# Attention and mixture-of-experts kernel: another order of score tiles, exponentials and routing tasks, and another buffer for one result

## The chip, the core and the metric

The kernel runs on one core of one Trainium2 chip, in a single launch. TensorE (PE) multiplies matrices into PSUM, ScalarE (ACT) applies tanh, exp, relu and casts, VectorE (DVE) and GpSimd (POOL) do elementwise work, and DMA queues are issued by SyncE (SP), ACT and POOL. The metric is the device time of the launch in microseconds (us); lower is better. A profile gives the span of one execution, engine by engine.

## The reference

Inputs are q, k, v of 8 batches x 12 heads x 448 tokens x 64, and a mixture of 8 experts over 3584 tokens of 768. All numbers are float32.

```
scores = cap * tanh((q @ k.T / 8) / cap)           # cap = 30
attn   = softmax(scores);  x = attn @ v            # 3584 x 768
logits = x @ w_gate;  e = argmax(logits)           # one expert for each token
out[t] = softmax(logits)[e] * (relu(x[t] @ w1[e]) @ w2[e])
```

## The kernel before

**Attention** works on pairs of heads. Step `n` of the loop (lines 1027 to 1059) takes pair `n` of 48; six steps are a batch, and two steps (an even one and the odd one behind it) share one load of q, k and v. The 448 keys of a pair are cut into three units of 128 and a rest of 64. The rests of an even pair and of the odd pair behind it fill one tile together, which the even step makes. `scores(n, half)` multiplies a unit's keys by the queries into a PSUM tile `sp` (L248; the rest at L260), of which there are two, so that a unit can't start before the tanh of the unit two ahead of it has ended. ACT puts the tanh into `pt` (L249) or, for the rest, into `pr` (L263), and then takes the exponential in place: units 0 and 1 at once (L266, 1792 columns), unit 2 alone (L266, 896 columns), the rest alone (L268). Half 0 is units 0 and 1; half 1 is unit 2 and, in even steps, the rest.

**Values.** `pv(n, half)` multiplies the exponentials by v into PSUM tiles `po0` (even pairs) and `po1` (odd pairs). It is called one step later than the scores: `pv(n-1, 0)` behind `scores(n, 0)`, and `pv(n-1, 1)` behind `scores(n, 1)`. For an even pair, its half 0 begins with the rest's matmuls for both pairs (L300), so in an odd step PE first does two units of scores, then L300, then L310 for units 0 and 1, then the sums of the softmax (L341), then unit 2, then L310 for unit 2. DVE copies `po` to `ot` (L319). `adds(n, half)` adds up the exponentials in `p4`: two additions on DVE (L277) and, for the rest, one on POOL (L285).

**Routing.** Behind each batch its softmax sums and its gate logits are worked off in the next batch's steps. With `n` the batch's last step plus one, a table of tasks (`at(step, when, f)`, L971 to L1022) says in which step and at which of the places 0, 5, 3, 6, 1, 2 of the loop's body each stands: `rec_v` (reciprocals, DVE), `rec_p` (PE, L396), `rec_c`, `log_v` (scaled logits `lr`, DVE, L410 to L424), `log_p` (PE, L429, sums them over partitions), `route_v` (first maximum and one-hot `ob`, DVE, L449 to L463), `route_s` (exp on ACT, L469), `place_p` (PE, L500 and L502), `route_g` (DVE, L474 to L481), `scale` and `store` of the rows into `xd` in DRAM, and `place_d`, which scatters token numbers (POOL, L527). The body's order is: loads, `turn`, 0, `scores(n, 0)`, `pv(n-1, 0)`, 5, `adds(n, 0)`, `scores(n, 1)`, 3, `pv(n-1, 1)`, 6, `adds(n, 1)`, 1, 2. Each engine runs its own instructions in the order written.

**The first expert block.** The largest expert's first block takes tokens of batches 0 to 3 only, so its rows are gathered from `xd` into `xg` during steps 37 to 43, three and one in turn and two at the end (L1007 to L1010, POOL, L750). DVE transposes them (`trans_x`, L858) from the end of step 44 on, and ACT and DVE split them into two parts.

**The experts.** Then come blocks in the order of `ORDER`: six of 448 tokens (large) and two of 256 (small). For each, `up` multiplies by w1 (L884), ACT and DVE make the hidden part `hb` (L889, L890), `down` multiplies by w2 (L908 large, L916 small), `evac` copies the sums from PSUM to `ys` (L934 large; L942 on ACT and L944 on DVE small), and `put` scatters `ys` to the output (POOL, L760). `ys` is one buffer for all blocks: `evac` of a block waits until the scatters of the block before have read it. For a small block all of the block before is scattered at once (L1257), 14 scatters if that one was large. The rows of the next block are gathered into `xg` while a block runs, transposed at its end, and `xg` has no further use after the last block's transposes.

Of the kernel before, what the change touches and what calls it, by code (L numbers as in the profile page):

```python
# [4 lines left out]
F32 = mybir.dt.float32  # L5
# [4 lines left out]
AF = mybir.ActivationFunctionType  # L10
# [15 lines left out]
KM = 384  # L26
# [98 lines left out]
def attention_moe(tc, qT, kT, vL, capd, wgL, w1a, w1b, w2a, w2b, cst, cmk, out):  # L125
# [110 lines left out]
    def scores(n, half):  # L236
        qr, kr, _ = raws[n // 2]
        i = n % 2
        if half == 0:
            probs[n] = pb.tile([128, 6, S], F32, name="pt", bufs=2)  # L240
        pt = probs[n]
        for g in (0, 1) if half == 0 else (2,):
            sp = ps_s.tile([128, 2, 512], F32, name="sp")
            c = slice(128 * g, 128 * g + 128)

            for j in range(2):
                r = slice(64 * j, 64 * j + 64)
                PE.matmul(sp[:, j, 0:S], kr[r, i, c], qr[r, i, :], start=True, stop=True)  # L248
            A.activation(out=pt[:, 2 * g : 2 * g + 2, :], in_=sp[:, 0:2, 0:S], func=AF.Tanh, scale=qsc)  # L249
            if n == g == 0:  # L250
                A.activation(out=pt[:, 0:2, :], in_=pt[:, 0:2, :], func=AF.Exp, scale=capt)
        rest = half == 1 and i == 0
        if rest:

            sp = ps_s.tile([128, 2, 512], F32, name="sp")
            pr = rests[n // 2] = pb.tile([128, 2, S], F32, name="pr", bufs=2)
            for i in range(2):
                for j in range(2):
                    r = slice(64 * j, 64 * j + 64)
                    PE.matmul(  # L260
                        sp[64 * i : 64 * i + 64, j, 0:S], kr[r, i, KM:S], qr[r, i, :], start=True, stop=True
                    )
            A.activation(out=pr, in_=sp[:, 0:2, 0:S], func=AF.Tanh, scale=qsc)  # L263

        for lo, hi in ((0, 4) if half == 0 else (4, 6),) if n else ((2, 4), (4, 6))[: 2 * half]:
            A.activation(out=pt[:, lo:hi, :], in_=pt[:, lo:hi, :], func=AF.Exp, scale=capt)  # L266
        if rest:
            A.activation(out=pr, in_=pr, func=AF.Exp, scale=capt)  # L268

# [20 lines left out]
    def pv(n, half):  # L290
# [3 lines left out]
        if half == 0 and n % 2 == 0:  # L294

            for i in range(2):
                pvs[n + i] = ps_o.tile([128, 512], F32, name=f"po{i}")
                r = slice(64 * i, 64 * i + 64)
                for j in range(2):
                    PE.matmul(  # L300
                        pvs[n + i][64 * j : 64 * j + 64, 0:S],
                        vr[r, 12 + j, :],
                        rests[n // 2][r, j],
                        start=True,
                        stop=False,
                    )
        po = pvs[n]
        for t in (0, 1) if half == 0 else (2,):
            for j in range(2):
                PE.matmul(  # L310
                    po[64 * j : 64 * j + 64, 0:S],
                    vr[:, n % 2 * 6 + 3 * j + t, :],
                    pt[:, 2 * t + j],
                    start=False,
                    stop=t == 2,
                )
# [609 lines left out]
    def evac(j, cs=range(2)):  # L926
        y = m["y"]
        if cs[0] == 0:
            ys[j] = ys0 if j < 0 else m["yo"].tile([128, QB * XW], F32, name="ys")
# [41 lines left out]
    for b in range(B):  # L971
# [13 lines left out]
        at(n + 3, 3, log_p, b)  # L985
        at(n + 3, 6, route_v, b)
        at(n + 4, 0, route_s, b)
        at(n + 4, 3, place_p, b)
        at(n + 4, 0, route_g, b)
# [37 lines left out]
    for n in range(n_pairs + 1):  # L1027
# [10 lines left out]
        if n > 0:  # L1038
            pv(n - 1, 0)
        do(n, 5)  # L1040
        if live:
# [3 lines left out]
            if n == 0:  # L1045
                adds(n, 0)
# [307 lines left out]
```

## Time and profile before

| | |
|---|---|
| median of three runs | 906.6 us (904.43 to 909.86) |
| the profiled execution | 905.34 us, of which the span is 903.6 us |
| mean granted clock of TensorE | 0.977 |
| VectorE busy | 548.7 us (61%) |
| ScalarE busy | 483.9 us (54%) |
| GpSimd busy | 466.0 us (52%) |

The span has three stages: attention up to about 340 us, a passage up to about 430 us in which attention's last steps overlap the first expert block, and the expert blocks up to the end. The expert blocks are ruled by TensorE; in attention TensorE and ScalarE are close to each other. Times in rows are microseconds from the span's start, a row being start, duration, engine, line, operation, output<-input, shapes and a count of merged instructions; what stands in brackets is the engine's idle time ahead of it and the instruction whose end released it.

### The profile page before, as it was taken

The page shows a single profiled execution, that of the slowest core. Times are in us where ns is not written, and L with a number is a line of the kernel's source. Part 1 is how long each engine was busy: PE and PEld are TensorE (multiplying, and loading weights), DVE is VectorE, ACT ScalarE, POOL GpSimd, SP SyncE. Part 2 cuts the span into 40 slices and gives each one's busy share as a digit, 9 for nine tenths or more (in the row PEclk, how much of TensorE's full clock was granted, in tenths as well). Part 3 has the DMA queues.
Part 4 walks back from the last instruction along what each step waited for, and adds up shares of the span by engine and source line. Part 5 has one row for each costly group of instructions (what it writes and reads, how often), then busy time and mean ns, then how long its engine had stood idle before and what let it go on. Part 6 is the DMA issues. An engine that isn't in the chain of part 4 may idle for free. (4 is left out here: it accounts for less than half of the span.)

```text
span 903.6 us, 12040 instructions
## 1 busy us (share of the span) xinstructions
PE 838.4 (93%) x4492; PEld 557.4 (62%) x4492; DVE 548.7 (61%) x885; ACT 483.9 (54%) x573; POOL 466.0 (52%) x382
## 2 busy tenths in 40 slices
PE   8999999999999996786999999999999999999893
PEld 3222322222223221265989989899999999999893
DVE  3559797979797965777373763744735537356520
ACT  7988889888978883632332532332423324234410
POOL 1423353434343645653718857577577575665600
PEclk9999999999999997998999999999999999999997
DMA  5231545454527572404455312453431124444100
GB/s 202 70 123 62 182 65 181 65 181 66 180 97 210 173 246 89 64 16 126 154 202 193 127 27 62 180 188 128 169 127 53 32 64 176 183 177 173 65 34 33
DMA packets 45155, 111.67 MB, mean 124 GB/s; under 512 B 8561, under 2 KB 27411, under 8 KB 42016
## 3 DMA queue, kind: packets, MB, share of 16 engines
q1 hardware_dynamic: 28384, 50.72, 19.6%
q0 software_dynamic: 16416, 59.87, 18.8%
q8 instruction: 37, 0.61, 0.3%
q14 instruction: 30, 0.25, 0.1%
q10 hardware_dynamic: 288, 0.23, 0.1%
HBM read 101.40 MB, written 22.36 MB: 137 GB/s over the span
## 5 line engine op out<-in xcount | busy, mean ns | idle before, releaser
L285 POOL TENSOR_TENSOR p<-p,pr 64x896 f32<-64x896 f32 x46 | 103.4, 2248 | 206.7 <-DVE p L277 150.3
L889 ACT ACTIVATE hb<-ph 128x448 fp32r<-128x448 f32 (+1 forms) x69 | 34.9, 508 | 296.7 <-PE ph L884 208.1
L890 DVE SCALAR_TENSOR_TENSOR hb<-ph,hb 128x448 fp32r<-128x448 f32 (+1 forms) x69 | 39.3, 574 | 202.6 <-ACT hb L889 202.5
L249 ACT ACTIVATE pt<-sp,qsc 128x896 f32<-128x896 f32 x144 | 138.7, 997 | 35.0 <-PE sp L248 34.9
L750 POOL DMA_INDIRECT xg<-xd,xi x114 | 134.5, 1180 | 37.9 <-issue 30.4
L248 PE MATMUL sp<-qr,kr 64*128 64x448 f32 x576 | 136.9, 580 | 11.1 <-ACT pt L249 10.9
L266 ACT ACTIVATE pt<-pt,capt 128x1792 f32<-128x1792 f32 (+1 forms) x96 | 134.9, 1406 | 2.3
L310 PE MATMUL po<-pt,vr 128*64 128x448 f32 x576 | 132.4, 568 | 0.0
L760 POOL DMA_INDIRECT out<-ys,xi x98 | 107.9, 1101 | 29.2 <-issue 27.0
L248 PEld LDWEIGHTS sp<-qr,kr 64*128 64x128 f32 x576 | 47.8, 187 | 98.7 <-ACT pt L249 43.7
L277 DVE TENSOR_TENSOR p<-pt 128x896 f32<-128x896 f32 x48 | 58.3, 1214 | 48.9 <-ACT pt L266 48.9
L310 PEld LDWEIGHTS po<-pt,vr 128*64 128x64 f32 x576 | 33.5, 138 | 76.4 <-issue 74.4
L277 DVE TENSOR_TENSOR p<-p,pt 128x896 f32<-128x896 f32 x48 | 53.8, 1121 | 9.6 <-ACT pt L266 9.5
L864 ACT CAST xh<-xt 128x448 fp32r<-128x448 f32 (+1 forms) x54 | 27.2, 532 | 42.6 <-DVE xt L858 42.6
L527 POOL DMA_INDIRECT ids<-tok,slots x32 | 38.4, 1200 | 10.9 <-issue 6.3
L319 DVE COPY ot<-po 128x448 f32<-128x448 f32 x48 | 29.7, 619 | 20.7 <-PE po L310 20.5
L300 PE MATMUL po<-pr,vr 64*64 64x448 f32 x192 | 25.0, 565 | 15.1 <-ACT pr L268 14.2
L750 POOL DMA_INDIRECT w1r<-in_w1b,widx x8 | 11.1, 1382 | 46.1 <-DVE w17l L796 45.5
L858 DVE STREAM_TRANSPOSE xt<-xg 128x448 f32<-128x448 f32 (+1 forms) x54 | 30.3, 585 | 7.3 <-DMA xg<-xd,xi 6.4
L865 DVE TENSOR_TENSOR xl<-xt,xh 128x448 fp32r<-128x448 f32 (+1 forms) x54 | 28.8, 559 | 2.6 <-ACT xh L864 2.5
L934 DVE STREAM_TRANSPOSE ys<-y 128x448 f32<-128x448 f32 x36 | 19.8, 612 | 12.8 <-DMA out<-ys,xi 7.3
L300 PEld LDWEIGHTS po<-pr,vr 64*64 64x64 f32 x192 | 5.3, 131 | 33.2 <-ACT pr L268 31.5
(410 smaller groups left out, 1970.6 us busy)
## 6 DMA issues: line engine op xcount, KB each, us to landing
vr<-in_vL SPq DMA_DIRECT2D x24, 448.0 KB, 6.2
kr<-in_kT SPq DMA_DIRECT2D x23, 448.0 KB, 3.7
qr<-in_qT SPq DMA_DIRECT2D x23, 448.0 KB, 6.0
xd<-yt SPq DMA_DIRECT2D x20, 336.0 KB, 6.8
xd<-w2r SPq DMA_DIRECT2D x12, 336.0 KB, 5.8
xg<-xd,xi POOLq DMA_INDIRECT x114, 3.1
out<-ys,xi POOLq DMA_INDIRECT x98, 2.4
w1r<-in_w1a SPq DMA_DIRECT2D x4, 384.0 KB, 6.2
```

Source lines behind the costliest of these rows:

```text
L248: PE.matmul(sp[:, j, 0:S], kr[r, i, c], qr[r, i, :], start=True, stop=True)
L249: A.activation(out=pt[:, 2 * g : 2 * g + 2, :], in_=sp[:, 0:2, 0:S], func=AF.Tanh, scale=qsc)
L266: A.activation(out=pt[:, lo:hi, :], in_=pt[:, lo:hi, :], func=AF.Exp, scale=capt)
L277: V.tensor_tensor(out=p4, in0=pt[:, 0:2] if half == 0 else p4, in1=pt[:, 2 * half + 2 : 2 * half + 4], op=ALU.add)
L285: e.tensor_tensor(out=p4[r], in0=p4[r], in1=rests[n // 2][r], op=ALU.add)
L300: PE.matmul(pvs[n + i][64 * j : 64 * j + 64, 0:S], vr[r, 12 + j, :], rests[n // 2][r, j], start=True, stop=False,)
L310: PE.matmul(po[64 * j : 64 * j + 64, 0:S], vr[:, n % 2 * 6 + 3 * j + t, :], pt[:, 2 * t + j], start=False, stop=t == 2,)
L527: i = G.indirect_dma_start(out=ids, out_offset=bass.IndirectOffsetOnAxis(ap=slots[0:p, c : c + 1].bitcast(U32), axis=0), in_=tok[0:p, c : ...
L750: G.indirect_dma_start(out=dst, out_offset=None, in_=src, in_offset=bass.IndirectOffsetOnAxis(ap=idx.bitcast(U32), axis=0), bounds_check=b ...
L760: i = G.indirect_dma_start(out=dst, out_offset=bass.IndirectOffsetOnAxis(ap=idx.bitcast(U32), axis=0), in_=src, in_offset=None, bounds_che ...
L889: A.activation(out=hh, in_=ph, func=AF.Relu)
L890: V.scalar_tensor_tensor(out=hl, in0=ph, scalar=0.0, in1=hh, op0=ALU.max, op1=ALU.subtract)
```

## The change

There are four edits.

1. `scores`: in even steps other than step 0 the rest's scores, tanh and exponential come ahead of those of unit 2. In step 0 each unit's exponential follows its tanh at once, and the order is 0, 1, 2, rest.
2. `pv(0, 0)` is done in step 0 behind its scores, not in step 1; for pair 0 alone the rest's matmuls come last.
3. In the table, `log_p` goes from place 3 to place 6 of its step (behind `pv(n-1, 1)`), `route_v` from 6 to 1 (behind `adds(n, 1)`), `route_s` from 0 to 5 and `route_g` from 0 to 6 of the step after.
4. `evac` of the first small block (`ORDER[-2]`) writes into `xg` in place of `ys`.

```diff
@@ scores
-        for g in (0, 1) if half == 0 else (2,):
+        rest = half == 1 and i == 0
+        units = (0, 1) if half == 0 else (2,) if not rest else (3, 2) if n else (2, 3)
+        for g in units:
             sp = ps_s.tile([128, 2, 512], F32, name="sp")
...
+            A.activation(out=x, in_=sp[:, 0:2, 0:S], func=AF.Tanh, scale=qsc)
+            if n == 0:
+                A.activation(out=x, in_=x, func=AF.Exp, scale=capt)
+        if n == 0:
+            return
         if rest:
+            pr = rests[n // 2]
             A.activation(out=pr, in_=pr, func=AF.Exp, scale=capt)
+        lo, hi = (0, 4) if half == 0 else (4, 6)
+        A.activation(out=pt[:, lo:hi, :], in_=pt[:, lo:hi, :], func=AF.Exp, scale=capt)
@@ pv
+        if n > 0 and half == 0 and n % 2 == 0:
+            rest()
+        main()
+        if n == 0 and half == 1:
+            rest()
@@ evac
-            ys[j] = ys0 if j < 0 else m["yo"].tile([128, QB * XW], F32, name="ys")
+            ys[j] = (
+                ys0
+                if j == -1
+                else xg.rearrange("p q x -> p (q x)")
+                if j == ORDER[-2]
+                else m["yo"].tile([128, QB * XW], F32, name="ys")
+            )
@@ the table
-        at(n + 3, 3, log_p, b)
-        at(n + 3, 6, route_v, b)
-        at(n + 4, 0, route_s, b)
+        at(n + 3, 6, log_p, b)
+        at(n + 3, 1, route_v, b)
+        at(n + 4, 5, route_s, b)
         at(n + 4, 3, place_p, b)
-        at(n + 4, 0, route_g, b)
+        at(n + 4, 6, route_g, b)
@@ the loop
-        if n > 0:
+        if n > 1:
             pv(n - 1, 0)
...
             if n == 0:
+                pv(n, 0)
                 adds(n, 0)
```

The change moves instructions on three engines that wait for one another. On ACT, step 2 and the first two tanh of step 3 stood so before (L249 is a tanh of units, L263 the rest's tanh, L266 an exponential of units, L268 the rest's):

```order
L249 ACTIVATE pt<-sp,qsc 128x896 x2
L266 ACTIVATE pt<-pt,capt 128x1792
L249 ACTIVATE pt<-sp,qsc 128x896
L263 ACTIVATE pr<-sp,qsc 128x896
L266 ACTIVATE pt<-pt,capt 128x896
L268 ACTIVATE pr<-pr,capt 128x896
L249 ACTIVATE pt<-sp,qsc 128x896 x2
```

The same even step 2 on ACT now, in which L263 is every tanh, L270 the rest's exponential and L272 that of units:

```order
L263 ACTIVATE pt<-sp,qsc 128x896 x2
L272 ACTIVATE pt<-pt,capt 128x1792
L263 ACTIVATE pr<-sp,qsc 128x896
L263 ACTIVATE pt<-sp,qsc 128x896
L270 ACTIVATE pr<-pr,capt 128x896
L272 ACTIVATE pt<-pt,capt 128x896
L263 ACTIVATE pt<-sp,qsc 128x896 x2
```

The rest's exponential, which PE's first value matmuls of step 3 read, has moved one place ahead of unit 2's, and PE's scores (L260, L248) have changed places with it.

On PE, the odd step in which batch 0's `log_p` stands (step 9) and the step behind it began so before, from the sums on (L341 sums, L248 scores, L429 `log_p`, L310 values):

```order
L341 MATMUL ps_s<-p_464,cs 32x448 x2
L248 MATMUL sp<-qr,kr 128x448 x2
L429 MATMUL ps_l<-lr,cs 128x112
L310 MATMUL po_562<-pt,vr 64x448 x2
L248 MATMUL sp<-qr,kr 128x448 x4
```

The same place on PE now (L357 sums, L252 scores, L319 values, L445 `log_p`):

```order
L357 MATMUL ps_s<-p_464,cs 32x448 x2
L252 MATMUL sp<-qr,kr 128x448 x2
L319 MATMUL po_562<-pt,vr 64x448 x2
L445 MATMUL ps_l<-lr,cs 128x112
L252 MATMUL sp<-qr,kr 128x448 x4
```

`log_p` has moved behind unit 2's value matmuls, and so stands directly ahead of the next step's scores.

On ACT at the end of the first small block, before and then now, with what each waits for (a DMASW is a semaphore of DMAs that POOL issues, a DMAHW one of DMAs that SP issues; L864 and L880 split the last block's rows, L889 and L905 make `hb`):

```order
L864 CAST xh<-xt 128x256 [waits DVE_49] x6
L942 COPY ys<-y_6534 128x3x4x32 [waits DMASW6_49,DMASW5_49,DMASW7_49,DMASW4_49,DMAHW4_49,DMASW3_49,DMAHW5_49,DMASW2_49,DMAHW6_49,DMASW1_49,DMAHW7_49,DMASW0_49,PE_49]
L942 COPY ys<-y_6536 128x3x4x32 [waits PE_49]
L889 ACTIVATE hb<-ph 128x256 [waits PE_49,Activation_49] x2
L791 CAST w17h<-w1r_115 128x768
```

```order
L880 CAST xh<-xt 128x256 [waits DVE_49] x6
L965 COPY xg<-y_6534 128x3x4x32 [waits DMASW2_49,DMASW1_49,DMASW7_49,DMASW0_49,PE_49]
L965 COPY xg<-y_6536 128x3x4x32 [waits DMASW5_49,DMASW4_49,DMASW6_49,DMASW3_49,PE_49]
L905 ACTIVATE hb<-ph 128x256 [waits PE_49,Activation_49] x2
L807 CAST w17h<-w1r_115 128x768
```

The first copy waited for twelve DMA semaphores in one row; each of the two copies now waits for four, as many as the gathers that filled its half of `xg` for the last block.

More of the change, by code (lines that the diff above doesn't have):

```diff
@@ L241, in scores @@
         pt = probs[n]
-        for g in (0, 1) if half == 0 else (2,):
+        rest = half == 1 and i == 0
+        units = (0, 1) if half == 0 else (2,) if not rest else (3, 2) if n else (2, 3)
+        for g in units:
             sp = ps_s.tile([128, 2, 512], F32, name="sp")
[L244 to L257, printed above, removed]
+            if g < 3:
+                c = slice(128 * g, 128 * g + 128)
                 for j in range(2):
                     r = slice(64 * j, 64 * j + 64)
[L260 to L263, printed above, removed]
@@ L265, in scores @@
-        for lo, hi in ((0, 4) if half == 0 else (4, 6),) if n else ((2, 4), (4, 6))[: 2 * half]:
-            A.activation(out=pt[:, lo:hi, :], in_=pt[:, lo:hi, :], func=AF.Exp, scale=capt)
+                    PE.matmul(sp[:, j, 0:S], kr[r, i, c], qr[r, i, :], start=True, stop=True)
+                x = pt[:, 2 * g : 2 * g + 2, :]
+            else:
+                for k in range(2):
+                    for j in range(2):
+                        r = slice(64 * j, 64 * j + 64)
+                        PE.matmul(
+                            sp[64 * k : 64 * k + 64, j, 0:S], kr[r, k, KM:S], qr[r, k, :], start=True, stop=True
+                        )
+                x = rests[n // 2] = pb.tile([128, 2, S], F32, name="pr", bufs=2)
@@ L297, in pv, with rest @@
                 pvs[n + i] = ps_o.tile([128, 512], F32, name=f"po{i}")
+        po = pvs[n]
+        def rest():
+            for i in range(2):
                 r = slice(64 * i, 64 * i + 64)
@@ L303, in pv, with main @@
                         rests[n // 2][r, j],
-                        start=True,
-                        stop=False,
-                    )
[L307 to L316, printed above, removed]
+                        start=n + i > 0,
+                        stop=n + i == 0,
+                    )
+        def main():
+            for t in (0, 1) if half == 0 else (2,):
+                for j in range(2):
+                    PE.matmul(
+                        po[64 * j : 64 * j + 64, 0:S],
+                        vr[:, n % 2 * 6 + 3 * j + t, :],
+                        pt[:, 2 * t + j],
+                        start=n == t == 0,
+                        stop=t == 2 and n > 0,
+                    )
+        if n > 0 and half == 0 and n % 2 == 0:
[3 more added lines that the diff above has]
+            rest()
         if half == 1:
@@ L928, in evac @@
         if cs[0] == 0:
-            ys[j] = ys0 if j < 0 else m["yo"].tile([128, QB * XW], F32, name="ys")
+            ys[j] = (
[4 more added lines that the diff above has]
+                else m["yo"].tile([128, QB * XW], F32, name="ys")
+            )
         o = ys[j]
```

## The prediction

> **What bounds the kernel now.** I begin with the busy time of each engine by stage (start:end, length, then PE, PE's weight loads, DVE, ACT and POOL, granted clock, share of the DMA engines, GB/s).
>
> ```profile
> 22.00:340.00 318.00, 303.45 (x1756) 92.44 (x1754) 250.16 (x388) 278.60 (x263) 131.62 (x73) 0.99 0.47 137
> 430.00:850.00 420.00, 415.11 (x2109) 383.81 (x2109) 220.99 (x333) 146.03 (x233) 276.20 (x266) 1.00 0.37 132
> ```
>
> PE is the bound in both: 303.45 of 318 us in attention, 415.11 of 420 us in the experts. ACT is close in attention (278.60). The change takes no matmul away, so it can only win PE's idle time: 14.55 us in attention, and what lies outside these stretches. Next, who ends PE's waits from 22 to 342 us (total, times, longest):
>
> ```profile
> PE po L300 <- ACT pr L268: 11.6, 22, 0.8
> PE ps_l L429 <- DVE lr L424: 2.0, 3, 0.7
> PE po L300 <- DVE ot L319: 0.9, 1, 0.9
> ```
>
> These three are 14.5 us, all of it. The large one stands once in every two steps: the rest's value matmuls wait for the rest's exponential. One such pair of steps, from the timelines of PE and ACT:
>
> ```profile
> 31.75 1.01 ACT L249 ACTIVATE pt<-sp,qsc 128x896 f32<-128x896 f32 x1 [0.96 <-PE sp L248]
> 38.66 1.77 PE L248 MATMUL sp<-qr,kr 64*128 64x448 f32 x8
> 39.12 1.04 ACT L266 ACTIVATE pt<-pt,capt 128x896 f32<-128x896 f32 x1
> 40.06 1.03 ACT L268 ACTIVATE pr<-pr,capt 128x896 f32<-128x896 f32 x1
> 41.14 0.98 PE L300 MATMUL po<-pr,vr 64*64 64x448 f32 x8 [0.71 <-ACT pr L268]
> 45.67 1.01 ACT L249 ACTIVATE pt<-sp,qsc 128x896 f32<-128x896 f32 x1 [0.97 <-PE sp L248]
> 46.45 1.77 PE L248 MATMUL sp<-qr,kr 64*128 64x448 f32 x8
> 48.16 1.73 PE L310 MATMUL po<-pt,vr 128*64 128x448 f32 x8
> ```
>
> The period, 31.75 to 45.67, is 13.92 us, a loop through both engines: ACT works without a gap from unit 2's tanh of the odd step (31.75) to the end of the rest's exponential (41.09), PE then needs until 45.67 to give it the next odd unit 2. Alone, each would be faster. Two units of scores take PE 1.71 us to their follower when nothing waits (46.45 to 48.16), here 2.48 (38.66 to 41.14): a wait costs 0.77, its printed 0.71 plus 0.06. So PE's own period is 13.15, and ACT's 13.92 - 0.96 = 12.96.
>
> **The change part by part.** *The rest ahead of unit 2.* Its exponential ends 0.94 us earlier (40.06 - 39.12), more than the longest wait (0.8 printed). The loop falls to 12.98, below PE's own 13.15, so PE paces. The second scores tile of the odd step now waits for unit 2's tanh; as the second of the two tanh it ends where the rest's did, so that wait is as long as before. ACT keeps 0.19 us of slack in a period: the whole wait goes, but only just. How far that holds, these rows of the same wait say:
>
> ```profile
> 280.75 0.98 PE L300 MATMUL po<-pr,vr 64*64 64x448 f32 x8 [0.44 <-ACT pr L268]
> 295.41 0.98 PE L300 MATMUL po<-pr,vr 64*64 64x448 f32 x8 [0.31 <-ACT pr L268]
> 310.01 0.98 PE L300 MATMUL po<-pr,vr 64*64 64x448 f32 x8 [0.77 <-ACT pr L268]
> 324.63 0.98 PE L300 MATMUL po<-pr,vr 64*64 64x448 f32 x8 [0.44 <-ACT pr L268]
> 339.40 1.11 PE L300 MATMUL po<-pr,vr 64*64 64x448 f32 x8 [0.31 <-ACT pr L268]
> 290.81 2.10 POOL L285 TENSOR_TENSOR p<-p,pr 64x896 f32<-64x896 f32 x1 [7.66 <-DVE p L277]
> 300.54 1.69 POOL L750 DMA_INDIRECT xg<-xd,xi  x1 [0.16 <-issue]
> 307.95 2.08 POOL L285 TENSOR_TENSOR p<-p,pr 64x896 f32<-64x896 f32 x1 [5.72 <-DMA xg<-xd,xi]
> 344.25 1.00 POOL L750 DMA_INDIRECT xg<-xd,xi  x1 [0.30 <-issue]
> 347.16 0.65 DVE L858 STREAM_TRANSPOSE xt<-xg 128x448 f32<-128x448 f32 x1 [6.44 <-DMA xg<-xd,xi]
> ```
>
> From step 37 (POOL's addition at 290.81) on, POOL alternates additions with the 14 gathers for the first expert block; the additions of odd steps wait until the gathers ahead have landed (5.72 us at 307.95). Its last gather is issued at 344.25, and DVE stands idle for 6.44 us until the rows are there at 347.16. So 290.81 to 347.16 (56.35 us) is a chain of POOL and DMA: what PE gains behind 291 us is lost in DVE's wait. The chain's start hangs on DVE's addition in step 37, which PE paces, so earlier gains pass. That leaves 22 waits less the last four: 11.6 - 0.31 - 0.77 - 0.44 - 0.31 = 9.8, and 18 x 0.06 = 1.1 beside them, **10.9 us**.
>
> *Unit 2's exponential later, and `log_p` later.* DVE's second addition of an even step now starts 0.8 to 0.9 us later, and three steps behind a batch DVE's `log_v` and PE's L429 follow it. The step of batch 1:
>
> ```profile
> 113.32 1.07 DVE L277 TENSOR_TENSOR p<-p,pt 128x896 f32<-128x896 f32 x1
> 114.16 0.98 PE L300 MATMUL po<-pr,vr 64*64 64x448 f32 x8 [0.31 <-ACT pr L268]
> 115.31 2.10 POOL L285 TENSOR_TENSOR p<-p,pr 64x896 f32<-64x896 f32 x1
> 115.52 2.77 DVE L419 TENSOR_TENSOR lt<-lt,rr 64x448 f32<-64x448 f32 x2
> 119.32 0.47 PE L429 MATMUL ps_l<-lr,cs 128*128 128x112 f32 x2 [0.69 <-DVE lr L424]
> 296.75 1.02 DVE L419 TENSOR_TENSOR lt<-lt,rr 64x448 f32<-64x448 f32 x2
> ```
>
> L419 takes 1.02 us alone and 2.77 beside POOL's addition: it ends 0.88 us after that does (118.29, 117.41). POOL's addition starts 0.17 us behind DVE's, here 115.4 instead of 115.31, because POOL was late anyway. So `lr` is ready at about 119.4 instead of 119.3. PE would reach the new place of L429 5.31 us after L300's start (41.14 to 46.45), and L300 starts at 113.79 without its wait: 119.10. A wait of about 0.3 stays of 0.75, in three batches: **+1.3 us** (at worst -0.3 each, at best +0.75 each). In batch 0, which had no wait, I expect POOL not late and so the 0.8 to 0.9 us to come through: a new wait of about 0.3, **-0.3** (ends 0 and -0.9). In step 33 DVE is behind for another reason:
>
> ```profile
> 249.97 1.31 PE L300 MATMUL po<-pr,vr 64*64 64x448 f32 x4 [0.91 <-DVE ot L319]
> 250.00:254.00 4.00, 4.00 (x12) 0.94 (x12) 3.95 (x6) 1.66 (x1) 2.07 (x1) 0.57 0.04 4
> ```
>
> PE waits until DVE has copied `po1`, so the 0.31 us won there is waited out again: **-0.4**. (The clock behind it was 0.57.) `route_v`, `route_s` and `route_g` stand behind instructions that others wait for, not ahead of them; what ACT waited for `route_s` lay in its slack of a period. I count nothing; the end is +0.5. In steps 45 to 47 DVE leads the passage: it no longer holds back an addition behind `route_v` but gets unit 2's exponential later in step 46; nothing, with ends -1 and +1.5.
>
> *Step 0.* ACT works without a gap there, and only the order in it changes: +0.2, ends 0 and 1.8 (PE's whole wait ahead of the first L300).
>
> *`xg` for `ys`.* The first small block's sums wait until 14 scatters of the large block before have read `ys`:
>
> ```profile
> 850.60 1.05 DVE L865 TENSOR_TENSOR xl<-xt,xh 128x256 fp32r<-128x256 f32 x3
> 851.97 0.28 PE L884 MATMUL ph<-xh,w10l 128*128 128x256 f32 x1
> 854.12 0.28 PE L884 MATMUL ph<-xh,w11l 128*128 128x256 f32 x1
> 856.79 0.86 ACT L942 COPY ys<-y 128x384 f32<-128x384 f32 x2 [5.67 <-DMA out<-ys,xi]
> 856.83 1.02 DVE L944 COPY ys<-y 128x384 f32<-128x384 f32 x2 [5.18 <-DMA out<-ys,xi]
> 858.00 0.67 PE L916 MATMUL y<-w20h,hb 128*128 128x384 f32 x1 [3.59 <-ACT hb L889]
> 858.00:862.00 4.00, 4.00 (x15) 4.00 (x16) 3.43 (x5) 2.40 (x4) 2.30 (x2) 0.57 0.41 162
> 858.00 3.92 PE y L916 x12
> 864.06 2.08 PE y L916 x12
> ```
>
> `xg` is free once the last block's rows are transposed, before 851.65 (the end of the splits). The copies then take DVE to 852.7, `hb` of the first `up` (matmuls until 852.25) is there by about 853.3, and PE, done with the second `up` at 854.24 (854.12 plus a matmul's spacing, 2.15 / 18 = 0.12), goes on at once: 858.00 - 854.24 = 3.76 us. After its wait the clock was 0.57, and twelve matmuls took 3.92 instead of 2.08: 1.84 more. What is late next is POOL's own pair of scatters, for which only the end waits, 30 us on. **5.6 us** in all; the lower end is 3.8.
>
> The Trainium skill, "TensorE: Matmul & The Clock Gate", Part 1: The HAM clock gate, says that the clock halves after an idle window of about 3.4 us and recovers after as long a busy one. The 3.59 us wait and the 0.57 agree. In step 33 the trace departs from it: waits of 0.31 and 0.91 us precede 0.57; by the page a short wait costs itself alone, and the sum would stay the same.
>
> The sum: 10.9 + 1.3 - 0.3 - 0.4 + 0.2 + 5.6 = 17.3 us, of 905.34 us for the profiled execution (span 903.6 and 1.74 around it): 888.0. The median of the runs is 1.3 higher, which gives 889.3; I say **888.6**.
>
> **The rivals.**
> *ACT takes the bound.* Its slack of 0.19 us a period is all there is: were its period 0.3 us over PE's, 18 periods would keep 5.4 us: 894. For: 278.60 busy of 318. Against: its waits for PE recur in every odd step.
> *POOL's gathers stretch or shrink.* Gathers took 1.69 us (300.54) or 1.00 (344.25). Were six more of the 14 slow because DVE is denser, 6 x 0.69 = 4.1 us come back: 892.7. Were the last rows to land 5 us sooner, PE would get most of DVE's 6.44: 884. The Trainium skill, "SBUF — State Buffer", SBUF: two separate sides, has a rule for the slow case: some DVE operations keep GpSimd from writing the descriptors of its own DMAs. The trace shows both durations but not which operation does it.
> *The chain doesn't move.* If its start hung on DMAs and not on DVE's step 37, attention's 11.7 would be lost: 900. Against: the row at 290.81 waited 7.66 us for DVE's addition, not for a DMA.
> *`xg` doesn't free the copies.* If the copies still waited for the scatters, 5.6 come back: 894. Against: they wait for fewer semaphores.
> *Slower.* L300 needs `po` copied by DVE. DVE's additions stand ahead of that copy and follow ACT, which now runs up to 0.8 us later against PE, so the copy could come late elsewhere, as in step 33. Price there: 0.91 us of wait and 4 us at a clock of 0.57, which lose 1.7: 2.6 us. From seven such steps on it eats 17.3 us; at fourteen, 36.4 - 17.3 = 19.1 slower, 926. Against: this wait stands once in 22 to 342 us.
>
> **How the numbers follow.** Forecast 0.66 (alone 884 to 893), ACT 0.10, gathers longer 0.06 or shorter 0.06, chain unmoved 0.05, copies not freed 0.04, slower 0.03. From 881 to 898 all but 900 and the slow case lie inside, with the ends of the unknown costs. A measurement of this kernel tells about 0.5% (4.5 us) from no change: only the last case is slower, a mishap of two of the others comes within: faster 0.94, same 0.03, slower 0.03.
>
> **What would show it.** PE's wait at L300 for the rest's exponential gone in all but the last steps, with the period at about 13.15; a wait of about 0.3 us at `log_p`; POOL's addition of step 37 near 279 us and still 56 us to the first transpose, DVE idle for 8 there; no wait of PE in the first small block and a clock of 1.00 behind it. The forecast fails if ACT's wait at odd unit 2 is gone while PE still waits, if POOL's 56 us change by over 4, or if PE waits for `ot` in more than one step.

## The result, and the profile after

The changed kernel takes **893.59 us** (median of 4 runs, 891.80 to 894.99), the kernel before in the same set 905.99 us (904.43 to 909.86): a ratio of 0.9847, 95% interval 0.9821 to 0.9872. The profiled execution takes 893.83 us with a span of 892.0, so 11.6 us of span are gone where the prediction had 17.3; by the medians it is 12.4. Line numbers have moved: scores L248 and L260 are now L252 and L259, the rest's values L300 are L308, the logits L355 are L371, `log_p` L429 is L445, `place_p` L500 is L516, the first expert block's transposes L858 are L874, `down` L908 and L916 are L924 and L932.

Who ends PE's waits from 20 to 335 us in the changed kernel (total, times, longest):

```profile
PE ps_l L516 <- DVE ob L479: 2.4, 5, 0.6
PE ps_l L371 <- DVE base L530: 2.1, 5, 1.2
PE ps_l L445 <- DVE lr L440: 2.1, 5, 1.0
PE po L308 <- DVE ot L335: 1.3, 1, 1.3
```

The wait for the rest's exponential, 11.6 us before, is not in the list any more. Two waits stand in it that before had nowhere in this stretch: `place_p` waits for the one-hot `ob` of `route_v`, and the logits wait until `place_v` has read the PSUM tile `ps_l` for `base`. PE's timeline shows them in their places; two rows of the rest's values without a wait stand ahead.

```profile
25.72 0.98 PE L308 MATMUL po<-pr,vr 64*64 64x448 f32 x8
38.86 0.98 PE L308 MATMUL po<-pr,vr 64*64 64x448 f32 x8
79.08 0.18 PE L516 MATMUL ps_l<-ob,mk 128*128 128x40 bf16 x1 [0.57 <-DVE ob L479]
116.04 0.47 PE L445 MATMUL ps_l<-lr,cs 128*128 128x112 f32 x2 [0.26 <-DVE lr L440]
122.18 0.18 PE L516 MATMUL ps_l<-ob,mk 128*128 128x40 bf16 x1 [0.44 <-DVE ob L479]
133.94 0.96 PE L371 MATMUL ps_l<-ot,wg 128*32 128x448 f32 x8 [0.22 <-DVE base L530]
159.22 0.47 PE L445 MATMUL ps_l<-lr,cs 128*128 128x112 f32 x2 [0.25 <-DVE lr L440]
242.19 1.31 PE L308 MATMUL po<-pr,vr 64*64 64x448 f32 x4 [1.29 <-DVE ot L335]
```

A plain pair of steps takes 38.86 - 25.72 = 13.14 us instead of 13.92. From `log_p` of one batch to the next, though, 43.18 us pass (116.04 to 159.22), not the 42.40 that the forecast gives for this batch (44.55 before, less three waits of the rest with what stands beside them, 0.83 + 0.51 + 0.38, and 0.43 of `log_p`'s). The difference of 0.78 is what stands between: 0.44 at `place_p`, 0.22 at the logits, and some 0.06 beside each.

Why `ob` comes late is read from DVE and POOL together, DVE's rows first:

```profile
117.43 1.09 DVE L281 TENSOR_TENSOR p<-p,pt 128x896 f32<-128x896 f32 x1
119.36 0.27 DVE L455 TENSOR_REDUCE tkm<-tkc 128x14 f32<-128x112 f32 x1
119.66 1.75 DVE L458 TENSOR_TENSOR tko<-kc,tkm 128x112 f32<-128x112 f32 x1
121.44 0.28 DVE L470 TENSOR_TENSOR ohm<-tko,cs 128x112 f32<-128x112 f32 x1
121.75 0.38 DVE L479 TENSOR_REDUCE ob<-ohm 128x32 bf16<-128x128 f32 x1
119.12 2.15 POOL L289 TENSOR_TENSOR p<-p,pr 64x896 f32<-64x896 f32 x1 [5.00 <-DVE df L467]
```

`route_v` now stands behind DVE's addition (117.43). POOL's addition reads what that one wrote. It starts 0.60 us behind its end, at 119.12 (the row names L467, which DVE had ended just before; why POOL is not sooner is not shown), and lasts to 121.27, and so runs in the middle of `route_v`: L458, which reads two tensors and took 0.28 in the kernel before, lasts until POOL has ended. The same happens in each of the five batches, to one instruction of `route_v` or another (1.75 to 1.87 us). The Trainium skill, "SBUF — State Buffer", Who interferes with whom, says that a DVE operation with both inputs in SBUF and a GpSimd operation that reads SBUF exclude each other for a whole instruction; this trace agrees, with about 1.5 us a batch. The reduction L455, with one input, passes beside POOL in 0.27.

The chain into the first expert block, and PE's wait behind it:

```profile
282.47 2.08 POOL L289 TENSOR_TENSOR p<-p,pr 64x896 f32<-64x896 f32 x1 [6.29 <-DVE p L281]
339.32 0.65 DVE L874 STREAM_TRANSPOSE xt<-xg 128x448 f32<-128x448 f32 x1 [6.46 <-DMA xg<-xd,xi]
341.53 1.86 PE L252 MATMUL sp<-qr,kr 64*128 64x448 f32 x4 [5.73 <-ACT pt L263]
404.18 0.67 PE L924 MATMUL z<-yt,w20h 128*128 128x448 f32 x2 [1.35 <-ACT w20h L807]
```

POOL's addition of step 37 comes 8.34 us sooner (290.81 before), the first transpose 7.84 us (347.16), the first `down` 8.47 us (412.65). Behind it, the lead stays until the small blocks:

```profile
812.27 0.65 PE L932 MATMUL y<-w20h,hb 128*128 128x384 f32 x2 [1.74 <-DVE hb L906]
817.80 0.34 PE L932 MATMUL y<-w21h,hb 128*128 128x384 f32 x1
844.95 0.86 ACT L965 COPY xg<-y 128x384 f32<-128x384 f32 x2
845.50 1.02 DVE L967 COPY xg<-y 128x384 f32<-128x384 f32 x2
852.42 0.34 PE L932 MATMUL y<-w21h,hb 128*128 128x384 f32 x1
848.00:853.00 5.00, 5.00 (x37) 5.00 (x37) 3.12 (x4) 2.90 (x5) 1.95 (x2) 1.00 0.43 165
812.00:817.00 5.00, 4.73 (x22) 4.73 (x23) 4.56 (x10) 1.51 (x3) 2.71 (x3) 0.66 0.19 49
```

The two copies of the first small block's sums (844.95, 845.50) wait for nothing now. The last two rows are the busy time by stage. Behind the last block's first `down`, where the prediction looked, the granted clock is 1.00; around the first small block's first `down` (812.27), ahead of which PE waits 1.74 us, it is 0.66. In the kernel before the same place had these rows:

```profile
819.89 0.62 PE L916 MATMUL y<-w20h,hb 128*128 128x384 f32 x2 [1.47 <-DVE hb L890]
823.88 0.34 PE L916 MATMUL y<-w21h,hb 128*128 128x384 f32 x1
863.90 0.34 PE L916 MATMUL y<-w21h,hb 128*128 128x384 f32 x1
819.90:825.00 5.10, 5.10 (x35) 5.10 (x36) 4.70 (x10) 2.38 (x5) 3.09 (x3) 1.00 0.30 72
```

The lead is 6.08 us at the first small block's `w21h` (823.88 - 817.80) and 11.48 at the last block's (863.90 - 852.42): 5.40 us come in between, from the copies.

### The profile page after: what moved, and what is told of

The parts are those of the page before. It is cut to its first block, busy times and chain, and to the rows that moved or that the text cites. A ratio compares the mean times of both kernels' runs of the same rounds, so it can differ in the third digit from the quotient of the medians.

```text
span 892.0 us, 12035 instructions
## 1 busy us (share of the span) xinstructions
PE 838.1 (94%) x4492; PEld 557.0 (62%) x4492; DVE 549.8 (62%) x885; ACT 484.1 (54%) x573; POOL 467.8 (52%) x382
## 4 chain that ended last, share of the span: by engine, by line
PE 42%; DVE 6%; issue 5%; DMA 5%; POOL 3%; ACT 2%; POOLq 0%; DVEq 0%; ACTq 0%
PE ph L900 21%; PE y L924 14%; PE y L932 4%; DMA out<-ys,xi 3%; DVE ys L957 1%; DMA xg<-xd,xi 1%; PE po L924 1%; PE z L924 1%; POOL out L776 1%; POOL p L289 1%; POOL xg L766 1%; DVE xl L881 1%; ACT pt L263 1%; ACT pt L272 1%; DVE yt L504 0%
## 5 line engine op out<-in xcount | busy, mean ns | idle before, releaser
L905 ACT ACTIVATE hb<-ph 128x448 fp32r<-128x448 f32 (+1 forms) x69 | 35.1, 509 | 298.3 <-PE ph L900 209.8
L263 ACT ACTIVATE pt<-sp,qsc 128x896 f32<-128x896 f32 x144 | 139.2, 1001 | 26.9 <-PE sp L252 23.6
L766 POOL DMA_INDIRECT xg<-xd,xi x114 | 131.5, 1154 | 41.9 <-issue 30.1
L252 PE MATMUL sp<-qr,kr 64*128 64x448 f32 x576 | 136.9, 580 | 11.3 <-ACT pt L263 10.9
L272 ACT ACTIVATE pt<-pt,capt 128x1792 f32<-128x1792 f32 x94 | 133.1, 1416 | 2.3
L319 PE MATMUL po<-pt,vr 128*64 128x448 f32 x576 | 132.6, 569 | 0.0
L252 PEld LDWEIGHTS sp<-qr,kr 64*128 64x128 f32 x576 | 47.6, 187 | 94.0 <-issue 45.4
L319 PEld LDWEIGHTS po<-pt,vr 128*64 128x64 f32 x576 | 33.6, 139 | 80.2 <-issue 78.7
L880 ACT CAST xh<-xt 128x448 fp32r<-128x448 f32 (+1 forms) x54 | 27.3, 533 | 42.3 <-DVE xt L874 42.3
L335 DVE COPY ot<-po 128x448 f32<-128x448 f32 x48 | 29.7, 618 | 11.8 <-PE po L319 11.6
L874 DVE STREAM_TRANSPOSE xt<-xg 128x448 f32<-128x448 f32 (+1 forms) x54 | 30.4, 586 | 8.0 <-DMA xg<-xd,xi 7.2
L259 PE MATMUL sp<-qr,kr 64*64 64x448 f32 x192 | 24.2, 572 | 3.6 <-ACT pt L263 3.6
L263 ACT ACTIVATE pr<-sp,qsc 128x896 f32<-128x896 f32 x24 | 23.9, 994 | 5.7 <-PE sp L259 5.1
```

What stands on the lines that cost most here:

```text
L263: A.activation(out=x, in_=sp[:, 0:2, 0:S], func=AF.Tanh, scale=qsc)
L319: PE.matmul(po[64 * j : 64 * j + 64, 0:S], vr[:, n % 2 * 6 + 3 * j + t, :], pt[:, 2 * t + j], start=n == t == 0, stop=t == 2 and n > 0,)
L766: G.indirect_dma_start(out=dst, out_offset=None, in_=src, in_offset=bass.IndirectOffsetOnAxis(ap=idx.bitcast(U32), axis=0), bounds_check=b ...
```

## The experiments

The runs came in sets, each on one chip, and the kernel before ran in each: 910.6 us in the first set (the first four runs), 919.8 in the second and 917.9 in the third (one chip for both), 921.2 in the last. Ratios are to the kernel before of the same set. Where intervals overlap, the traces are compared by three marks that come ahead of the disturbance told of under the last run:

| kernel | `log_p` of batch 1 to that of batch 2 | POOL's addition, step 37 | first `down` | ratio (interval) |
|---|---|---|---|---|
| before | 44.55 | 290.81 | 412.65 | 1 |
| only `xg` for `ys` | 44.56 | 291.36 | 414.04 | 0.9943 (0.9919 to 0.9967) |
| `xg`, new table, old order of the rest | 43.61 | 287.96 | 410.00 | 0.9955 (0.9919 to 0.9991) |
| only the rest first | 44.24 | 288.81 | 417.35 | 0.9985 (0.9963 to 1.0007) |
| changed, old table | 44.24 | 288.33 | 416.94 | 0.9923 (0.9892 to 0.9953) |
| changed, `log_p` at its old place | 44.10 | 286.11 | 414.61 | 0.9933 (0.9906 to 0.9960) |
| changed, `route_*` at their old places | 43.66 | 283.73 | 407.39 | 0.9883 (0.9841 to 0.9925) |
| changed | 43.18 | 282.47 | 404.18 | 0.9847 (0.9821 to 0.9872) |
| changed, second set | 43.36 | 281.49 | 403.23 | 0.9903 (0.9866 to 0.9940) |
| changed, places later | 42.38 | 278.89 | 401.69 | 0.9765 (0.9727 to 0.9803) |
| the same, third set | 42.40 | 277.00 | 398.28 | 0.9855 (0.9801 to 0.9909) |
| changed, odd additions on DVE | 43.17 | 283.10 | 400.17 | 0.9844 (0.9804 to 0.9884) |
| both | 42.38 | 279.00 | 394.95 | 0.9800 (0.9752 to 0.9847) |

How far a mark can be trusted is seen where the code up to it is the same. The batch time then agrees within 0.2 us (43.18, 43.36, 43.17; 42.38, 42.40, 42.38). POOL's addition of step 37 differs by up to 2.0 us even inside one set (277.00 and 279.00 in the third), and most of that comes behind one wait in step 33, which is told of in the last section. The first `down` of the kernel with the places later differs by 3.4 us between two sets (401.69 and 398.28). So a difference of 2 us at step 37, or of 3 at the first `down`, says little by itself.

**`xg` for `ys` alone.** The kernel before with edit 4.

```diff
-            ys[j] = ys0 if j < 0 else m["yo"].tile(...)
+            ys[j] = ys0 if j == -1 else xg... if j == ORDER[-2] else m["yo"].tile(...)
```

> The kernel before with the fourth edit alone (first small block's sums into xg). Theory: PE's wait of 3.59 us behind the second up of the last block goes, and with it the slow clock behind it; 5.4 us less than before (ratio about 0.994), nothing else moves. Rival: the write into xg brings a wait of its own, or the low clock seen in the changed kernel at the start of the first small block (0.66) comes from this edit: then that dip is here too and the gain is 4 us or less (0.996 or more).

Measured: 0.9943, which is 5.2 us of the set's 910.6 (3.0 to 7.4), and PE's wait ahead of the last block's sums is gone. The low clock at the start of the first small block isn't there either, so it doesn't come from this edit. The edit's term is confirmed by itself.

**The rest first, alone.** The kernel before with edit 1 from step 2 on.

```diff
-        for g in (0, 1) if half == 0 else (2,):
+        units = (0, 1) if half == 0 else (2,) if not rest else (3, 2) if n else (2, 3)
+        for g in units:
...
```

> The kernel before with the rest ahead of unit 2 in even steps from step 2 on, nothing else. Theory: PE's waits for the rest's exponential go (11.6 us to under 0.5), but PE then waits for the scaled logits at the old place of log_p, 1.0 to 1.2 us in each of batches 0 to 3, and not at place_p; POOL's addition of step 37 starts 7 to 8.5 us earlier than before (290.81), ratio about 0.991. Rival: the waits at place_p (0.45 to 0.57 us a batch in the changed kernel) come from PE being faster and not from the table: then they are here too, on top of those at log_p.

Measured: 0.9985, no difference that the interval tells from none. PE's waits up to 335 us in this kernel (where `log_p` is L431 and the logits are L357):

```profile
PE ps_l L431 <- DVE lr L426: 6.5, 5, 1.9
PE ps_l L357 <- DVE base L516: 3.3, 6, 0.7
PE po L302 <- DVE ot L321: 1.3, 1, 1.3
```

The rest's wait is gone here too, but DVE gets unit 2's exponential later and is late for `log_p` and the logits. PE gets only 2.0 us of lead by step 37 (290.81 - 288.81), and at the first `down` it is 4.7 us behind. `place_p` doesn't wait here, but the logits wait for `base` already, with the table of before: the new order alone brings that wait. The expectation was wrong: the order of the rest earns almost nothing by itself.

**The changed kernel with the table of before.**

```diff
-        at(n + 3, 6, log_p, b)
-        at(n + 3, 1, route_v, b)
-        at(n + 4, 5, route_s, b)
+        at(n + 3, 3, log_p, b)
+        at(n + 3, 6, route_v, b)
+        at(n + 4, 0, route_s, b)
...
-        at(n + 4, 6, route_g, b)
+        at(n + 4, 0, route_g, b)
```

> The changed kernel with the table of before (log_p at 3, route_v at 6, route_s and route_g at 0). Theory: no wait at place_p nor for base at the gate logits, 1.0 to 1.2 us at log_p in batches 0 to 3 instead of 0.26; together about 0.1 to 0.3 us a batch worse than the changed kernel, so POOL's addition of step 37 at 282.5 to 284 and a time within 0.2% of the changed kernel (0.984 to 0.987). Rival: the table's edits are what holds attention back: without them step 37 comes at 280 and the time is 3 us less (0.981).

Measured: 0.9923 against 0.9847, with the same waits as in the run before (6.5 and 3.3 us). Set against the first comparison, the four moves of the table are worth about 0.8% on top of the new order, not 0.2%; the two figures are from two sets.

What the two kernels lose behind step 37 is not in the waits of attention. From POOL's addition of step 37 to the first `down` they take 128.5 and 128.6 us, and the kernel with `log_p` alone at its old place (further down) 128.5; the nine others in which POOL does all its additions take 121.3 to 123.7, the kernel before 121.8. So the new order with the old place of `log_p` loses 6 to 7 us in the passage. About half of it is seen at the `log_p` of batch 7: PE waits there 1.9 to 2.2 us at 400 to 403 us, and over the 5.5 us behind it the granted clock is 0.69, where the changed kernel waits 0.22 us and has 1.00. The other half is not traced.

**`place_p` and `place_v` later.** If the wait at `place_p` is the missing term, then giving DVE one group of value matmuls more should bring it.

```diff
-        at(n + 4, 3, place_p, b)
+        at(n + 4, 6, place_p, b)
...
-        at(n + 5, 1, place_v, b)
+        at(n + 5, 6, place_v, b)
```

> The changed kernel with place_p one place later (6 instead of 3, behind the values of unit 2) and place_v ahead of the second addition of its step (6 instead of 1). Theory: the waits at place_p (2.4 us in five batches) and for base at the gate logits (2.1 us) go, nothing takes their place, POOL's addition of step 37 starts about 3 us earlier (279.5 instead of 282.47), time about 890.5 (0.981 to 0.982). Rival: ACT, with 0.19 us of slack a period, or DVE takes over: step 37 stays at 282 and the time within 0.1% of the changed kernel.

Measured: 0.9765, clear of the changed kernel's interval in the first comparison. The waits left up to 335 us:

```profile
PE ps_l L445 <- DVE lr L440: 2.0, 5, 1.0
PE po L308 <- DVE ot L335: 1.3, 1, 1.3
PE ps_l L371 <- DVE base L530: 0.2, 1, 0.2
PE ps_s L357 <- POOL p L289: 0.2, 1, 0.2
```

A batch takes 42.38 us, as the forecast had it for the changed kernel (42.40), and POOL's addition of step 37 stands where the prediction put it:

```profile
278.89 2.09 POOL L289 TENSOR_TENSOR p<-p,pr 64x896 f32<-64x896 f32 x1 [6.30 <-DVE p L281]
```

**The changed kernel again**, beside the next three.

> The changed kernel itself once more, beside the three below on one chip, so that they are compared with it and not with a figure of another chip. Expected: 0.985 of the kernel before, PE waits of 2.4 us at place_p, 2.1 at the logits and 2.1 at log_p between 20 and 335 us.

Measured: 0.9903, nearer to 1 than in the first comparison. The waits in attention are of the same kind: 2.8 us at `place_p`, 1.4 at the logits, 2.0 at `log_p`. Why the gain is smaller is taken up under the last run. This trace also settles what makes `place_p` wait, for in batch 2 it doesn't:

```profile
163.36 0.28 DVE L470 TENSOR_TENSOR ohm<-tko,cs 128x112 f32<-128x112 f32 x1
163.37 2.21 POOL L289 TENSOR_TENSOR p<-p,pr 64x896 f32<-64x896 f32 x1 [5.85 <-DVE tko L458]
165.07 0.19 PE L516 MATMUL ps_l<-ob,mk 128*128 128x40 bf16 x1
```

POOL's addition starts here as the last instruction of `route_v` with two inputs in SBUF is already running, and that one takes 0.28 us. In the other four batches one of them takes 1.87 to 2.08 us beside POOL's, and `place_p` waits 0.56 to 0.78. The place of `route_v` behind DVE's addition is the same in all five, so the wait needs POOL's addition inside `route_v`, and the place alone doesn't make it. The kernel with the new table and the old order of the rest, further down, shows the same: where an instruction of `route_v` takes 1.80 to 2.21 us beside POOL's addition, in three batches, `place_p` waits 0.48 to 0.84, and in the two where POOL's comes later it doesn't wait.

**Odd additions on DVE.** This tests the chain behind step 37.

```diff
-            e = V if n >= n_pairs - 2 else G
+            e = V if n >= n_pairs - 2 or n in (39, 41, 43) else G
```

> The changed kernel with the three odd additions of the rest in steps 39, 41 and 43 on DVE instead of POOL. Theory (the passage into the first expert block is set by a chain of POOL and DMA: POOL's additions stand 4 to 7 us between the gathers): without them the last of the 14 gathers is issued 4 to 6 us sooner, DVE's wait for xg falls from 6.5 us to under 2, PE's from 5.7 to under 2, first down near 399 instead of 404, 4 to 5 us less (0.990 of the changed kernel, 0.5 to 0.6%). Rival (the gathers' landing or the data they wait for sets the passage, not POOL's additions): DVE still waits over 5 us for xg, no gain, or a loss of up to 2 us from three additions of 1.1 us on DVE.

Measured: the first transpose on DVE, and PE's first two waits behind it:

```profile
333.84 0.64 DVE L874 STREAM_TRANSPOSE xt<-xg 128x448 f32<-128x448 f32 x1
339.85 0.47 PE L445 MATMUL ps_l<-lr,cs 128*128 128x112 f32 x2 [1.88 <-DVE lr L440]
346.57 1.77 PE L259 MATMUL sp<-qr,kr 64*64 64x448 f32 x8 [2.89 <-ACT pt L263]
```

From POOL's addition of step 37 to the first transpose 50.74 us pass (283.10 to 333.84) instead of 55.50 in this set's changed kernel (56.85 in the first), DVE doesn't wait for `xg`, and PE's 5.7 us ahead of L252 are gone. A wait of 1.88 at `log_p` and one of 2.5 for POOL's sums (at 358.78) take some of it back: the first `down` comes 3.1 us sooner than in the changed kernel of this set. By time the ratio falls by 0.006, as expected, though the intervals just overlap. So three of POOL's additions were 5 to 6 us of that chain, and the landing of the rows didn't set it. What would set the rest isn't shown, for DVE doesn't wait for the rows any more.

**`log_p` alone at its old place.**

```diff
-        at(n + 3, 6, log_p, b)
+        at(n + 3, 3, log_p, b)
```

> The changed kernel with log_p alone back in its place of before; route_v, route_s and route_g stay where the change puts them. Theory 1 (DVE's chain lr, route_v, ob sets when place_p can go, so a wait at log_p is only an earlier part of the one at place_p): waits at log_p rise from 0.26 to about 1.1 us in five batches (+4.4 us), the waits at place_p (2.4 us) go, net 2 us slower, 0.2%. Rival (the later log_p is what the table's whole 11 us of the profiles are): 6 to 11 us slower, 0.7 to 1.2%.

Measured, waits up to 335 us:

```profile
PE ps_l L445 <- DVE lr L440: 6.5, 5, 1.9
PE ps_l L371 <- DVE base L530: 1.8, 5, 0.6
PE po L308 <- DVE ot L335: 1.3, 1, 1.3
PE ps_l L516 <- DVE ob L479: 1.2, 3, 0.6
```

Two more rows have 0.7 us at `place_p`. The waits at `log_p` are those of theory 1 (1.13 to 1.16 us in four batches, 1.93 in the fifth). It had also said that those at `place_p` would go, and they don't: 1.9 us are left of the 2.8 in the same set's changed kernel. POOL's addition (121.48) still runs inside `route_v`, whose L470 takes 2.20 us there instead of 0.28. A batch takes 0.7 us more than in the same set's changed kernel (44.10, 43.36), and the first `down` comes 11.4 us later, which is the rival's size; 4.6 of them are there at step 37 (286.11 for 281.49), the rest is lost in the passage as above. The time, 0.3% slower with overlapping intervals, doesn't decide between them.

**`log_p` alone at its new place.**

```diff
-        at(n + 3, 1, route_v, b)
-        at(n + 4, 5, route_s, b)
+        at(n + 3, 6, route_v, b)
+        at(n + 4, 0, route_s, b)
...
-        at(n + 4, 6, route_g, b)
+        at(n + 4, 0, route_g, b)
```

> The changed kernel with route_v, route_s and route_g back in their places of before and log_p alone in its new place. Theory 1 (route_v behind an addition on DVE is what makes PE wait at place_p): the wait for ob goes, log_p waits 0.26 us as in the changed kernel, 2 us faster than the changed kernel, 0.2%. Rival (the moves of route_v and route_s are what the table gains, since before them DVE's additions and ACT's tanh wait): POOL's addition of step 37 comes 3 us later or more than in the changed kernel's 282.5, and the kernel is 3 to 8 us slower, 0.3 to 0.9%.

Measured, waits up to 335 us:

```profile
PE ps_l L371 <- DVE base L530: 3.8, 6, 0.8
PE ps_l L445 <- DVE lr L440: 2.0, 5, 1.0
PE po L308 <- DVE ot L335: 1.3, 1, 1.3
```

The wait for `ob` is gone, as theory 1 said: with `route_v` ahead of the addition, POOL's comes after it (121.63, when `ob` was written at 120.12) and L458 takes 0.28. But the logits now wait 0.63 us on average (3.8 / 6) instead of 0.2, and a batch takes 43.66. POOL's addition of step 37 comes 2.2 us later and the first `down` 4.2 us later than in the same set's changed kernel: what is saved at one place is paid at the next, and more. The time (0.9883) doesn't tell it from the changed kernel (0.9903). The larger part of the table's gain is `log_p`'s: of the 12.8 us at the first `down` between the old table and the new one (416.94 to 404.18), `log_p` alone brings 9.5 (to 407.39), `route_*` alone 2.3 (to 414.61). These marks are of three sets, and about half of `log_p`'s share is the passage.

**The new table with the old order of the rest.** The kernel before with edits 3 and 4 alone; the diff is the `+` lines of edit 3.

> The kernel before with xg for ys and with the table's four moves, but with the rest behind unit 2 as before. It is the fourth corner of a square: old order and old table 0.9943, new order and old table 0.9923, both new 0.985. Theory (log_p's later place is needed because the new order gives lr 0.9 us later; with the old order there is little to win): the 21 waits at the rest's value matmuls stay at 11.3 us, the waits at log_p (3.0 us) go, first down near 411, 1 to 3 us faster than old order and old table, 0.991 to 0.993. Rival (the table alone brings what new order and table bring together): first down before 407, 0.988 or less.

Measured: 0.9955, with an interval around that of `xg` alone. The rest's wait stays (8.4 us in 18 waits up to 335), the one at `log_p` goes, and `place_p` waits 1.8 us here too, the logits 1.2. That misses the expected 0.991 to 0.993, in a set where edit 4 has less to win (last run). By the first `down`, which was expected near 411, the square reads: table alone 4.0 us sooner than the `xg` kernel (410.00 for 414.04), order alone (the changed kernel with the old table) 2.9 later, both 9.9 sooner. In attention, though, the two just add: a batch gains 0.95 us by the table, 0.32 by the order, and 1.20 to 1.38 by both. So what they earn only together, by these marks, is the passage, where the order alone loses; the corners are of three sets.

**Both: places later, and odd additions on DVE.** First the places alone once more in this set, then both.

> The changed kernel with place_p behind the first value matmuls and place_v one place later, once more, beside the next on one chip. Theory: 0.977 of before as on the other chip, no wait at place_p, POOL's addition of step 37 at 279. Rival (what it won was that chip's): 0.985, as the changed kernel.

> Both together: place_p and place_v later, and the odd additions of steps 39, 41 and 43 on DVE. Theory (the first shortens the steps up to 37, the second the chain behind it, so they add): first down near 397 to 399 instead of 401.7, 3 to 5 us less than with the first alone, 0.971 to 0.974 of before. Rival (the second's gain is the same idle time of PE that the first has already taken): as the first alone, 0.976 to 0.978.

Measured: 0.9855 and 0.9800. The first is the figure that its rival gave. But on this chip the changed kernel itself had 0.9903; a batch takes 42.40 us as in the first set, and `place_p` doesn't wait, so by the trace the gain is there. By time it isn't told from the changed kernel's. Both together are the shortest of the set (899.69 us for 917.9), with the first `down` at 394.95, 3.3 us sooner than with the places alone. From step 37 to the first transpose 48.76 us pass instead of 54.82. By these marks the two edits add, as expected; the levels of both ratios are higher than expected, and by time they overlap (0.55% apart). The interval of both together lies clear of the changed kernel's in the second set (0.9866 to 0.9940), as that of the places alone did in the first.

**The kernel before, for its trace.** The traces of the second and third sets had a standstill in the last two blocks.

> The kernel before, for its trace on another chip. In the runs beside which it took 918 to 920 us, all the kernels tried showed 6 to 8 us in the last two blocks in which PE stood with nothing in the trace that it waited for. Theory (this belongs to the chip and the moment, not to the change): where before takes 915 us or more, its trace has the same standstill behind 820 us, and the stretch from the last large block's first w20h to the end is 142 us or longer instead of 137.8. Rival (only the changed kernels have it): 137 to 139 us there, without such waits, at any time of the whole. On a chip with before near 906 this tells nothing.

Measured: 921.4 us (917.5 in the execution of the trace). From the last large block's first `w20h` to the end 150.3 us pass, against 141.1 in the first trace of this kernel (the expectation's 137.8 is not this stretch of that trace). PE's waits from 820 to 866 us:

```profile
PE ph L884 <- issue: 4.0, 6, 1.0
PE y L916 <- DVE hb L890: 2.1, 1, 2.1
PE y L916 <- issue: 1.7, 5, 0.4
```

and the copies that edit 4 frees:

```profile
868.88 0.86 ACT L942 COPY ys<-y 128x384 f32<-128x384 f32 x2
869.27 1.01 DVE L944 COPY ys<-y 128x384 f32<-128x384 f32 x2
```

So the standstill isn't the change's: PE stands for 5.7 us in this kernel too, with nothing in the trace that it waits for. And while it stands, the scatters end: the copies that waited 5.67 and 5.18 us in the first trace wait for nothing here. From the first small block's first `w20h` to the end the traces without the standstill take 85.7 and 86.3 us without edit 4 and 80.1 to 82.0 with it; those with the standstill take 95.0 (this one) without and 90.4 to 94.4 with it. So edit 4 wins less there, about 1 to 5 us, going by one trace without it. That fits the step of the changed kernel from 0.9847 to 0.9903, but wasn't tried by itself, and the kernel with the places later moved by more (0.9765 to 0.9855). What causes the standstill stays open.

## Why the prediction was right, and where it wasn't

The change is faster, as forecast, by 12.4 us where the prediction gave 17.3. Three rivals had given times nearer to 893.6 than its 888.6: ACT as the bound (894), copies not freed (894) and longer gathers (892.7). None came about: PE waits for ACT nowhere between 20 and 335 us, the copies wait for nothing, and the 14 gathers took 15.9 us in all instead of 18.3.

- **The rest ahead of unit 2 (10.9 us): right in its mechanism.** The wait at the rest's values is gone in all steps, the period is 13.14 (13.15 forecast), and PE paces it: ACT waits 0.17 us for PE at unit 2 of the odd step (43.38), where 0.19 of slack was forecast. With the places moved, step 37 comes 11.9 us sooner (290.81 - 278.89), against the 11.7 that attention's terms sum to; that it is so close is partly luck, for the same kernel in the third set has 277.00.
- **`log_p` (+1.3 in three batches, -0.3 in batch 0): right.** The wait that stays is 0.25 to 0.26 (0.3 forecast), also in batch 0. But the text priced this move against the old order only. With the old table the new order brings 2.0 to 2.5 us by step 37, not 10.9, and with `log_p` alone at its old place 4.7 (286.11): much of the first term hangs on the table's moves, and this was not seen.
- **Step 33 (-0.4): right.** The wait for `ot` is 1.29, and 0.91 + 0.31 = 1.22 was expected.
- **Step 0 (+0.2): not told.** At the rest's values of pair 2 the lead is 27.22 - 25.72 = 1.50 us, of which 0.77 is that wait: 0.7 for step 0. But the same attention code reached that place at 27.22, 27.38 and 28.33 in three traces.
- **The failing step, first part: `route_v`, `route_s` and `route_g` "stand behind instructions that others wait for, not ahead of them ... I count nothing".** It asked who stands behind the moved instructions in their queue, and not who waits for what they write. `place_p` waits for `ob`: 0.57, 0.44, 0.45, 0.44 and 0.48 us in five batches, 2.4 us. With `route_v` at its old place this wait is gone, and in batches where POOL's addition misses `route_v` it is gone too. The prediction had the mechanism in hand, for it used L419's 2.77 us beside POOL's addition, and didn't ask which of `route_v`'s instructions would come beside one.
- **The failing step, second part: "the whole wait goes".** The prediction asked for ACT and for `log_p` whether they keep up with a PE that no longer waits, and not for `place_v` on DVE. The logits wait for its `base`: 0.22, 0.21, 0.22 and 0.18 us up to step 37, 0.8 us. The order of the rest alone brings this wait (3.3 us in six waits up to 335 us), the new table alone too (1.2 us in two), and the run with `place_v` ahead of the second addition is without it up to step 37.
- **The sum to step 37.** The two parts are 3.2 us, and nine times 0.06 beside them 0.5: 11.7 + 0.5 (step 0) - 3.2 - 0.5 = 8.5, measured as 8.34. At this mark equal code differs by up to 2.0 us, so the agreement within 0.2 is luck.
- **The chain of 56 us: right.** 56.85 were measured, and the run with the odd additions on DVE shows that three additions were 5 to 6 us of it. Only DVE's idle time was off: 8 us were forecast, 6.46 measured, and 6.54 also with the places later and the whole lead; why is open.
- **`xg` (5.6 us): right**, 5.40 in the trace and 5.2 alone by time. The wait that it named is gone, and "a clock of 1.00" held behind it. But "no wait of PE in the first small block" did not hold: PE waited there 1.47 us for `hb` before and 1.74 (812.27) now, the clock behind it fell to 0.66, and the lead from that block's first `w20h` (817.91 before, 810.01 after) to its `w21h` fell from 7.90 to 6.08. This -1.8 was in no term.
- **Together:** 8.34 at step 37, some 0.4 lost until the small blocks, -1.8 and +5.4 there, make 11.5 of the 11.6 us.

## What to carry to other kernels

When a task is moved, ask two questions of each engine: who stands behind it in the queue, and who waits for what it writes; and look at what its new neighbours on other engines do to its own duration. A wait that ends last is usually one of several that end within a microsecond, so an edit that removes it earns only as much as the next one leaves; here the order of the rest alone was not told from nothing by time (0.9985). Compare the timeline at a few fixed marks along the kernel and not only the total, for a disturbance at the end can hide or take an edit's gain; and see first by how much a mark differs between runs of equal code.

## What the runs showed of the hardware

- **The clock and short waits.** A wait of 1.74 us at the first small block was followed by a clock of 0.66 over 5 us in the changed kernel; a wait of 1.73 us at the same place in the run of `xg` alone, and of 1.47 before, were followed by 1.00. In step 33 PE waits 1.28 to 1.29 us for `ot` in the changed kernel and in those with the places later or the additions moved: over the 7 us from 1 us behind it the clock is 0.79, 0.77, 0.76 and 0.76 in four of these traces and 1.00 in the two others, and the stretch from there to the rest's next values takes 1.3 to 1.6 us longer at the low clock. The Trainium skill, "TensorE: Matmul & The Clock Gate", Part 1: The HAM clock gate, gives an idle window of about 3.4 us; here less than that was enough in some traces, and the same length was not in others. What decides is not in these traces.
- **A standstill of PE without a cause in the trace**, in the small blocks at the end: 5.7 us in the last trace of the kernel before and 6 to 8 in six of the seven others of the second and third sets. In the seventh, that of `log_p` alone at its old place, it is 1.9, and PE waits 5.8 more for an instruction of ACT ahead of which ACT stood 9.6 us, with nothing on this core that it waited for. None of the traces of the first set or of the first comparison has it.
